# FNet mixing gated by a GLU: another load position for tiles five to eight, and other places for statistics, the fourth tile's turn and normalisations in the first block

## The chip, the cores and the metric

The kernel runs on one core of one Trainium2 chip. The metric is the device time of one execution in microseconds (us), and of several executions the median. The core has a matrix engine (TensorE, PE in the profile, with its weight loads as PEld), a vector engine (VectorE, DVE), a scalar engine (ScalarE, ACT), GpSimd (POOL) and SyncE (SP), which issues most of the loads. Each engine works through its own list of instructions in order and waits on semaphores for the others.

## The reference, cut to what matters

```python
x = A_x                                   # 1 x 2048 x 512
xn = _layernorm(x, axis=-1)
a = einsum("bsd,ed->bse", xn, dft_hid_re)
b = einsum("bsd,ed->bse", xn, dft_hid_im)
s = einsum("ts,bse->bte", dft_seq_re, a) - einsum("ts,bse->bte", dft_seq_im, b)
h = sigmoid(xn @ w_gate) * (xn @ w_up)    # 512 -> 1792
g = silu(h @ w_down)                      # 1792 -> 512
return x + s * g
```

## The kernel before, in words

The 2048 rows of x are 16 tiles of 128 rows, in two halves of eight (`KH` is 8). The 1792 hidden columns are seven groups of 256. The kernel goes over the halves and, inside each, over the groups; then come the sequence transform and the hidden transform. Every fp32 operand is split into a rounded part ("hi", written by ACT) and the rest ("lo", written by DVE), and a product is three matmuls: hi by hi, hi by lo and lo by hi.

The change lies in the first block, the function `start`, which handles the first half and the first group while its eight tiles are still coming in. All its instructions are put out by `begin`, in an order written by hand; each engine takes its own in that order. The matter of the first block is this:

- `fetch(i)` allocates a page for tiles i and i+1 and has SP load both. With `hold=True` DVE first writes one word into the page, so that the load waits until DVE has come to that point of its list.
- `loads[0]` and `loads[1]` are the first and the second weights, 512 KB each. `w_hi(f, j)` and `w_lo(f, j)` split them for feature half f.
- `norm_a(i)` computes a tile's statistics: two instructions on DVE (L155, L156) and two small ones on POOL (L157, L158). `norm_b(i)` normalises the tile with them on DVE (L163).
- `turn(i)` transposes a normalised tile with four instructions on PE (L176) into one of two "pd" banks. `keep_hi(i)` (ACT, L195), `keep_lo(i)` (DVE, L201) and `keep_raw(i)` (ACT, L187) take it out of the bank, in that order. So `turn(i)` waits for `norm_b(i)` and for `keep_raw(i - 2)`, which frees the bank.
- `chunk(q, f, order, between)` multiplies tiles 2q and 2q+1 with feature half f: three passes of eight matmuls of 256 columns (L553). It needs both tiles' hi parts for its first pass, their lo parts for another, the weights' lo parts for the third. `between` is run among the passes.
- `next_tile(i)` turns tile i, takes it out of its bank, and prepares later tiles.
- `gated(b, f)` is a sigmoid on ACT (L566) and a product on DVE (L567), put out when the two chunks of 512 rows are done; the function that it returns splits the result (ACT L273, DVE L274) and is called one chunk later as `left`.
- Four operand splits of the following block (ACT L66, DVE L67, and two sums at L118) are put among the last chunks.

The loop over the chunks, where most of the order is set, reads before the change:

```python
for q in range(4):
    for f in range(2):
        if f == 0:
            chunk(q, f, ((0, 0), (1, 0), (0, 1)))
            next_tile(2 * q + 2)
        else:
            chunk(q, f, ((0, 0), (0, 1), (1, 0)), lambda: next_tile(2 * q + 3))
        if left:
            left()
        left = gated(q // 2, f) if q % 2 else None
```

Tiles are counted from 0 in the code, so tile 3 is the fourth, and tiles five to eight are i = 4 to 7.

Of the kernel before, what the change touches and what calls it, by code (L numbers as in the profile page):

```python
# [20 lines left out]
KH = NS // NH  # L21
# [10 lines left out]
def fnet_glu_kernel(ctx: ExitStack, tc: tile.TileContext, x, x_t, c_re, c_im, w_h, w_gu, w_down, out):  # L32
# [9 lines left out]
    def page(shape, dtype=F32R):  # L42
        return pages.tile([P, *shape], dtype, name="page")

    def bank(tag):
        return banks.tile([P, 512], F32, name=tag, bufs=2 if tag == "pd" else 1)
# [77 lines left out]
    units = []  # L124
# [7 lines left out]
    def after(n, f):  # L132
        extra.setdefault(n, []).append(f)
# [7 lines left out]
    def fetch(i, hold=False):  # L141
        pg = page([2, D], F32)
        if hold:
            nc.vector.memset(pg[:, 0, :1], 0.0)
        for j in range(2):
            xs[i + j] = pg[:, j, :]
            nc.sync.dma_start(xs[i + j], x[(i + j) * P : (i + j + 1) * P, :])
# [3 lines left out]
    def norm_a(i):  # L151
        st = stat.tile([P, 6], F32, name="st")
        mv = stat.tile([P, 2], F32, name="mv")
        rs = stat.tile([P, 2], F32, name="rs")
        nc.vector.bn_stats(st, xs[i])  # L155
        nc.vector.bn_aggr(mv, st)  # L156
        nc.gpsimd.tensor_scalar(rs[:, 0:1], mv[:, 1:2], EPS, None, op0=ALU.add)  # L157
        nc.gpsimd.tensor_tensor(rs[:, 1:2], rs[:, 0:1], mhalf, op=ALU.pow)  # L158
        st_of[i] = mv, rs

    def norm_b(i):
        mv, rs = st_of.pop(i)
        nc.vector.tensor_scalar(xs[i], xs[i], mv[:, 0:1], rs[:, 1:2], op0=ALU.subtract, op1=ALU.mult)  # L163
# [9 lines left out]
    def turn(i):  # L173
        turned[i] = bank("pd").rearrange("p (d s) -> p d s", d=ND)
        for d in range(ND):
            nc.tensor.transpose(turned[i][:, d, :], xs[i][:, d * P : (d + 1) * P], ident)  # L176

    def place(i):
        h, b, o = i // 8, i % 8 // 4, i % 4
        return [(h, j, b) for j in range(2)], slice(o * P, (o + 1) * P)  # L180

    def keep_raw(i):
        keys, at = place(i)
        for j, k in enumerate(keys):
            if k not in xraw:
                xraw[k] = page([2, SB], F32)
            nc.scalar.activation(xraw[k][:, :, at], turned[i][:, 2 * j : 2 * j + 2, :], AF.Copy)  # L187

    def keep_hi(i):
        keys, at = place(i)  # L190
        for j, (h, _, b) in enumerate(keys):
            k = h, XK[j, b]
            if xop[k].at is None:
                xop[k].at = page([2, SB]), page([2, SB])
            nc.scalar.activation(xop[k].at[0][:, :, at], turned[i][:, 2 * j : 2 * j + 2, :], AF.Copy)  # L195

    def keep_lo(i):
        keys, at = place(i)
        for j, (h, _, b) in enumerate(keys):
            hi, lo = xop[h, XK[j, b]].at  # L200
            nc.vector.tensor_tensor(lo[:, :, at], turned[i][:, 2 * j : 2 * j + 2, :], hi[:, :, at].bitcast(F32), op=SUB)  # L201
# [3 lines left out]
    def x_sum(h, k):  # L205

        if (h, k) not in xsum:
            xsum[h, k] = page([2, SB], F32)
        a, b = {
            1: lambda: (xraw[h, 0, 1], xraw[h, 0, 0]),  # L210
            2: lambda: (xraw[h, 1, 1], xsum[h, 1]),
            3: lambda: (xraw[h, 1, 1], xraw[h, 0, 1]),
            4: lambda: (xraw[h, 1, 0], xsum[h, 2]),
        }[k]()
        nc.vector.tensor_tensor(xsum[h, k], a, b, op=SUB)
# [54 lines left out]
    def finish(h, hs, b, f, s):  # L270
        pg = page([2, SB])
        hs[f, b] = pg[:, 0, :], pg[:, 1, :]
        nc.scalar.activation(pg[:, 0, :], s, AF.Copy)  # L273
        return lambda: nc.vector.tensor_sub(pg[:, 1, :], s, pg[:, 0, :].bitcast(F32))  # L274
# [251 lines left out]
    def start(h, g):  # L526

        loads = [Load(w_gu[g, k], [2, 4 * P]) for k in range(2)]
        wdl = Load(w_down[g], [2, D])
        wd = [Parts([wdl], lambda f=f: wdl.load()[:, f, :], [D], joint=True) for f in range(2)]  # L530
        w, hs, ps = {}, {}, {}

        def w_hi(f, j):
            k, o = QUAD[f, j]
            both = page([2, 4 * P])
            w[f, j] = both[:, 0], both[:, 1]
            nc.scalar.activation(both[:, 0], loads[k].load()[:, o, :], AF.Copy)

        def w_lo(f, j):
            k, o = QUAD[f, j]  # L540
            nc.vector.tensor_tensor(w[f, j][1], loads[k].load()[:, o, :], w[f, j][0].bitcast(F32), op=SUB)

        def chunk(q, f, order, between=None):
            b, a = divmod(q, 2)
            if a == 0:
                for m in range(2):
                    ps[b, f, m] = bank("gu"[m] + ("bc", "ab")[b][f])
            at = slice(a * 2 * P, (a + 1) * 2 * P)
            for n, (u, v) in enumerate(order):
                for m in range(2):  # L550
                    for d in range(ND):
                        o = (2 * m + d % 2) * P
                        nc.tensor.matmul(  # L553
                            ps[b, f, m][:, at],
                            w[f, d // 2][u][:, o : o + P],
                            xop[h, XK[d // 2, b]].at[v][:, d % 2, at],
                            start=n == d == 0,
                            stop=n == 2 and d == ND - 1,
                            skip_group_check=True,
                        )  # L560
                if n == 0 and between is not None:
                    between()

        def gated(b, f):
            s = page([SB], F32)
            nc.scalar.activation(s, ps[b, f, 0], AF.Sigmoid)  # L566
            nc.vector.tensor_mul(s, s, ps[b, f, 1])  # L567
            return lambda: finish(h, hs, b, f, s)()

        def begin():  # L570
            idle = bank("gc")

            def busy(times, wide):
                for _ in range(times):
                    nc.tensor.matmul(idle[:, :wide], ones[:, :P], ones[:, :wide], start=True, stop=True)

            busy(10, 512)
            fetch(0)
            loads[0].load()
            norm_a(0)  # L580
            fetch(2, hold=True)
            loads[1].load()
            fetch(4)
            fetch(6)
            for p in units[0][0] + units[2][0]:
                p.load()
            wdl.load()
            norm_a(1)
            w_hi(0, 0)
            norm_b(0)  # L590
            turn(0)
            busy(2, 256)
            keep_hi(0)
            norm_b(1)
            turn(1)
            busy(4, 256)
            keep_hi(1)
            w_hi(0, 1)
            w_lo(0, 0)
            norm_a(2)  # L600
            w_lo(0, 1)
            norm_a(3)
            for i in range(2):
                keep_lo(i)
            w_hi(1, 0)
            w_hi(1, 1)
            norm_b(2)
            for i in range(2):
                keep_raw(i)
            w_lo(1, 0)  # L610
            norm_b(3)
            w_lo(1, 1)

            def next_tile(i):
                if i >= KH:
                    return
                turn(i)
                keep_hi(i)
                if 3 < i + 1 < KH:
                    norm_b(i + 1)  # L620
                keep_lo(i)
                if i + 2 < KH:
                    norm_a(i + 2)
                keep_raw(i)

            left = None
# [3 lines that stand above are left out]
                        chunk(q, f, ((0, 0), (1, 0), (0, 1)))  # L630
                        next_tile(2 * q + 2)
                    else:
                        chunk(q, f, ((0, 0), (0, 1), (1, 0)), lambda: next_tile(2 * q + 3))
                    if left:
                        left()
                    left = gated(q // 2, f) if q % 2 else None
                    n = 2 * q + f - 3
                    if 0 <= n < 4:
                        units[0 if n < 2 else 2][0][2 + n % 2].get()
            left()  # L640
            x_sum(h, 1)
            x_sum(h, 2)
            after(0, lambda: x_sum(h, 3))
            after(0, lambda: x_sum(h, 4))

        return (h, g, hs, wd), begin
# [313 lines left out]
    with tc.manual_schedule():  # L960
# [3 lines left out]
        for h in range(NH):  # L964
            n = len(units)
# [12 lines left out]
            if h == 0:  # L978
                n = len(units)
# [81 lines left out]
```

## Time and profile before

| what | value |
|---|---|
| median of 3 runs | 821.85 us (821.62 to 821.89) |
| the profiled execution: time, span | 822.36 us, 820.6 us |
| PE busy in the span | 809.8 us (99%) |
| DVE, ACT, POOL busy | 645.2, 490.9, 144.0 us |
| PE busy in the first 10, second 10, third 10 us | 8.08, 8.83, 9.25 us |
| granted PE clock | 0.999 |

The profiled execution is 0.51 us longer than the median of the runs and 1.76 us longer than its own span, which runs from the first to the last instruction. A row of the timeline gives the start in us, the length in us, the engine with line, operation and tiles, how many instructions are merged into it, and in brackets how long the engine had been idle and what ended that. The length of a matmul is modelled and overlaps the next one; the distance between starts tells the rate. A row of the chain of waits gives start, length and the work on the path to the end.

### The profile page before, as it was taken

The numbers are of one execution on the slowest core, as the hardware profiler recorded it, in microseconds if no ns is written. First come the engines' busy times: TensorE is split into PE (matmuls) and PEld (weight loads), VectorE is DVE, ScalarE is ACT, GpSimd is POOL, SyncE is SP. The second block draws the span as 40 slices with busy tenths as digits, with TensorE's granted clock in tenths as the row PEclk, the third lists the DMA queues.
The fourth block names the chain that finished last, engine by engine and source line by source line (L and its number), as shares of the span: only waits on it lengthen the run. The fifth ranks groups of instructions, "written<-read, shape, count | busy, mean of one in ns | idle before, by whom it ended". The sixth has DMA issues, their size and how long they took to land.

```text
span 820.6 us, 10472 instructions
## 1 busy us (share of the span) xinstructions
PE 809.8 (99%) x3686; PEld 673.2 (82%) x3686; DVE 645.2 (79%) x814; ACT 490.9 (60%) x762; POOL 144.0 (18%) x214
## 2 busy tenths in 40 slices
PE   8999999999999999999999999999999999999997
PEld 7988888888878888888888888888888888888786
DVE  6798867757788867876797796889888976988946
ACT  4666655655677888887787773544355545535441
POOL 2143422322111122212121100011101110002201
PEclk9999999999999999999999999999999999999999
DMA  8349999699677888998999997358937994799984
GB/s 317 144 170 401 272 257 285 186 321 309 163 175 165 228 179 214 251 200 199 280 291 311 265 347 271 134 209 309 310 146 287 341 394 150 253 316 395 304 275 77
DMA packets 59253, 207.27 MB, mean 253 GB/s; under 512 B 6592, under 2 KB 6848, under 8 KB 59200
## 3 DMA queue, kind: packets, MB, share of 16 engines
q0 software_dynamic: 25072, 87.57, 42.1%
q1 hardware_dynamic: 34128, 119.03, 40.2%
q8 instruction: 29, 0.48, 0.2%
q14 instruction: 24, 0.20, 0.1%
HBM read 122.16 MB, written 88.08 MB: 256 GB/s over the span
## 4 chain that ended last, share of the span: by engine, by line
PE 93%; DVE 3%; ACT 1%; DMA 1%; issue 1%; POOL 0%; SPq 0%; DVEq 0%
PE pd L70 6%; PE pd L71 6%; PE pd L72 6%; PE ga L70 5%; PE ga L72 5%; PE ua L72 5%; PE ua L71 5%; PE ga L71 5%; PE ua L70 5%; PE gc L70 3%; PE gc L72 3%; PE gc L71 3%; PE uc L72 3%; PE uc L70 3%; PE uc L71 3%; PE gb L72 3%
## 5 line engine op out<-in xcount | busy, mean ns | idle before, releaser
L67 DVE TENSOR_TENSOR page<-page 128x1024 fp32r<-128x1024 f32 (+1 forms) x340 | 322.0, 978 | 116.0 <-ACT page L66 114.5
L66 ACT ACTIVATE page<-page 128x1024 fp32r<-128x1024 f32 (+1 forms) x340 | 276.1, 859 | 91.8 <-DVE page L118 72.1
L118 DVE TENSOR_TENSOR page<-page 128x1024 f32<-128x1024 f32 (+2 forms) x184 | 169.2, 935 | 8.0 <-DMA page<-xn_part 5.9
L291 ACT ACTIVATE page<-pd 128x512 f32<-128x512 f32 x154 | 89.5, 595 | 62.7 <-PE pd L72 59.4
L295 POOL DMA_DIRECT2D g_part<-page x69 | 60.1, 889 | 277.2 <-ACT page L291 220.6
L70 PE MATMUL pd<-page 128*128 128x512 f32 x242 | 94.3, 390 | 0.8 <-DVE page L898 0.8
L71 PE MATMUL pd<-page 128*128 128x512 f32 x242 | 94.2, 389 | 0.0
L72 PE MATMUL pd<-page 128*128 128x512 f32 x242 | 94.2, 389 | 0.0
L70 PE MATMUL ga<-page 128*128 128x512 f32 x200 | 78.1, 391 | 0.8 <-ACT page L308 0.8
L72 PE MATMUL ga<-page 128*128 128x512 f32 x200 | 77.9, 390 | 0.0
L72 PE MATMUL ua<-page 128*128 128x512 f32 x200 | 77.9, 390 | 0.0
L71 PE MATMUL ga<-page 128*128 128x512 f32 x200 | 77.9, 389 | 0.0
L70 PE MATMUL ua<-page 128*128 128x512 f32 x200 | 77.9, 389 | 0.0
L71 PE MATMUL ua<-page 128*128 128x512 f32 x200 | 77.9, 389 | 0.0
L70 PEld LDWEIGHTS pd<-page 128*128 128x128 f32 x242 | 45.4, 188 | 10.7 <-issue 1.2
L72 PEld LDWEIGHTS pd<-page 128*128 128x128 f32 x242 | 45.4, 188 | 9.4
L71 PEld LDWEIGHTS pd<-page 128*128 128x128 f32 x242 | 45.4, 188 | 9.4
L70 PE MATMUL ub<-page 128*128 128x512 f32 (+1 forms) x126 | 48.3, 383 | 0.5 <-DVE page L940 0.5
L70 PE MATMUL gc<-page 128*128 128x512 f32 x124 | 48.6, 392 | 0.0
L71 PE MATMUL gc<-page 128*128 128x512 f32 x124 | 48.3, 390 | 0.0
L72 PE MATMUL gc<-page 128*128 128x512 f32 x124 | 48.3, 389 | 0.0
L70 PE MATMUL uc<-page 128*128 128x512 f32 x124 | 48.3, 389 | 0.0
(135 smaller groups left out, 1351.9 us busy)
## 6 DMA issues: line engine op xcount, KB each, us to landing
g_part<-page POOLq DMA_DIRECT2D x77, 512.0 KB, 7.8
page<-in_c_re_dram SPq DMA_DIRECT2D x36, 512.0 KB, 6.3
page<-f_part SPq DMA_DIRECT2D x36, 512.0 KB, 5.5
page<-in_c_im_dram SPq DMA_DIRECT2D x34, 512.0 KB, 6.0
page<-in_w_gu_dram SPq DMA_DIRECT2D x28, 512.0 KB, 7.6
f_part<-page POOLq DMA_DIRECT2D x28, 512.0 KB, 6.9
page<-in_w_down_dram SPq DMA_DIRECT2D x14, 512.0 KB, 8.7
page<-xn_part SPq DMA_DIRECT2D x14, 512.0 KB, 8.4
```

What stands on the lines that cost most here:

```text
L66: nc.scalar.activation(hi, src, AF.Copy)
L67: nc.vector.tensor_tensor(lo, src, hi.bitcast(F32), op=SUB)
L70: nc.tensor.matmul(ps, ws[0], ms[0], start=first, stop=False, skip_group_check=go_on)
L71: nc.tensor.matmul(ps, ws[0], ms[1], start=False, stop=False, skip_group_check=go_on)
L72: nc.tensor.matmul(ps, ws[1], ms[0], start=False, stop=last, skip_group_check=go_on)
L118: (engine or nc.vector).tensor_tensor(dst, a, b, op=op)
L291: nc.scalar.activation(pg[:, o, :], po, AF.Copy, scale=float(sign))
L295: nc.gpsimd.dma_start(g_part[i], pg, accum_op=ADD)
```

## The change

- The loads of tiles 4 to 7 move behind `norm_a(2)` and are held by DVE. With them move the loads behind them on SP's list: the two weights of the next group and the down weights (512 KB each).
- `norm_a(3)` moves behind `norm_b(2)`, and `norm_b(3)` behind both `w_lo` of the second weights.
- In the first chunk of feature half 1 the fourth tile's turn stands behind the second pass and no longer behind the first. In the later chunks of that half the turn stays behind the first pass.
- `norm_b(4)` to `norm_b(7)` leave `next_tile` and stand at the end of the loop's body, behind `left` and `gated`.

```diff
@@ chunk
             for n, (u, v) in enumerate(order):
+                if n and n - 1 in (between or {}):
+                    between[n - 1]()
...
-                if n == 0 and between is not None:
-                    between()
@@ begin
             loads[1].load()
-            fetch(4)
-            fetch(6)
-            for p in units[0][0] + units[2][0]:
-                p.load()
-            wdl.load()
             norm_a(1)
...
             norm_a(2)
+            for i in (4, 6):
+                fetch(i, hold=True)
+            for p in units[0][0] + units[2][0]:
+                p.load()
+            wdl.load()
             w_lo(0, 1)
-            norm_a(3)
...
             for i in range(2):
                 keep_raw(i)
+            norm_a(3)
             w_lo(1, 0)
+            w_lo(1, 1)
             norm_b(3)
-            w_lo(1, 1)
@@ next_tile
                 keep_hi(i)
-                if 3 < i + 1 < KH:
-                    norm_b(i + 1)
                 keep_lo(i)
@@ the loop
-                        chunk(q, f, ((0, 0), (0, 1), (1, 0)), lambda: next_tile(2 * q + 3))
+                        chunk(q, f, ((0, 0), (0, 1), (1, 0)), {int(q == 0): lambda: next_tile(2 * q + 3)})
...
                     left = gated(q // 2, f) if q % 2 else None
+                    if 3 < 2 * q + f + 3 < KH:
+                        norm_b(2 * q + f + 3)
```

## The prediction

> **What bounds the kernel now.** I read the chain that ended last, then PE's own waits over the whole run (those after the first, which is ahead of all work), then the timeline of the first block.
>
> ```profile
> PE 93%; DVE 3%; ACT 1%; DMA 1%; issue 1%; POOL 0%; SPq 0%; DVEq 0%
> ```
>
> ```profile
> PE pd L70 <- DVE page L898: 0.8, 1, 0.8
> PE ga L70 <- ACT page L308: 0.8, 1, 0.8
> PE pd L176 <- DVE page L163: 0.7, 1, 0.7
> PE gb L553 <- DVE page L201: 0.6, 1, 0.6
> PE pd L176 <- ACT page L187: 0.6, 1, 0.6
> PE ub L70 <- DVE page L940: 0.5, 1, 0.5
> ```
>
> PE is the bound almost everywhere. What any order of the first block can change is PE's waiting there; whatever PE loses or gains before about 37 us moves all that follows. Three waits lie where the change works: 0.6 on the lo parts (L201), 0.6 on a bank freed by ACT (L187), 0.7 on a normalised tile (L163). The change must remove these, and it may put new ones in their place.
>
> **The first two waits.** Timeline rows of the first 14 us, then rows of the chain and one of the page's groups that give PE's rate:
>
> ```profile
> 1.64 0.42 SPq L81 DMA_DIRECT2D page<-in_w_gu_dram  x1
> 5.05 0.43 SPq L81 DMA_DIRECT2D page<-in_w_gu_dram  x1
> 5.53 1.87 SPq L147 DMA_DIRECT2D page<-in_x_dram  x4
> 6.49 0.63 ACT L537 ACTIVATE page<-page 128x512 fp32r<-128x512 f32 x1 [4.26 <-DMA page<-in_w_gu_dram]
> 9.40 0.68 DVE L155 BATCH_NORM_STATS2 st<-page 128x6 f32<-128x512 f32 x1
> 10.22 1.39 DVE L201 TENSOR_TENSOR page<-pd,page 128x256 fp32r<-128x256 f32 x4
> 11.32 0.83 PE L553 MATMUL gb<-page 128*128 128x256 f32 x4 [0.60 <-DVE page L201]
> 11.45 1.15 ACT L537 ACTIVATE page<-page 128x512 fp32r<-128x512 f32 x2 [2.73 <-DMA page<-in_w_gu_dram]
> 11.52 0.54 DVE L163 TENSOR_SCALAR page<-page,mv,rs 128x512 f32<-128x512 f32 x1
> 13.20 0.66 PE L176 MATMUL pd<-ident,page 128*128 128x128 f32 x4 [0.57 <-ACT page L187]
> ```
>
> ```profile
> 19.08 0.48 PE gb L553 x4
> 19.56 0.48 PE ub L553 x4
> 37.66 0.23 PE ga L71
> ```
>
> ```profile
> L71 PE MATMUL pd<-page 128*128 128x512 f32 x242 | 94.2, 389 | 0.0
> ```
>
> A pass of eight takes 0.96. A matmul's row is longer than its share of PE's time: 389 ns against 0.23.
>
> Without norm_a(3) ahead of them, the lo parts start at 9.40 where L155 stood, not at 10.22: 0.82 earlier, more than the 0.60 that PE waited for them. That wait goes. The two held pages put two one-word writes into DVE's list; they fall where DVE waits for ACT's split of the first weights, so I cost them at nothing (if that cover is gone, no more than twice the 0.18 of L156, below).
>
> The turn at 13.20 waited for ACT: second weights landed 11.45, two splits, then the copies that free the bank, 1.75 in all. So this turn stands at the landing plus 1.75, or where PE and norm_b(2) allow it. PE alone allows 13.20 - 0.60 - 0.57, less 0.16 twice, because a row's modelled end hangs over by 0.389 - 0.23: 11.71. norm_b(2) moves up by the same 0.82, to 10.70, and ends at 11.24. The landing is the unknown. The first weights, with nothing issued behind them, took 6.49 - 1.64 = 4.85 from issue to use; the second, with the four tiles issued right behind, 11.45 - 5.05 = 6.40. The bounds are 9.90 and 11.45. I take 9.90, because the changed list gives the second weights the surroundings of the first: SP issues nothing more until DVE reaches the held pages' writes, about 0.8 ahead of the L155 at 9.40, at about 8.6. Then the turn comes at about 11.7, **1.5 earlier**; at the other end nothing is gained.
>
> [...]
>
> The tiles' loads go out from about 8.7, not 5.53.
>
> ```profile
> DMA to landing us min/median/max: 2.5/6.7/8.4
> ```
>
> By this row of L147 tile 4 lands between 11.2 and 17.1; DVE wants it for norm_a(4) at about 14.5. Only the rest of the second weights is ahead of it, so I take the lower half and no cost; at 17.1 it would cost 1.2 (DVE's 2.6 less what PE still has queued). The next weights and the down weights slip by some 3 us and are first split among the last chunks (L66): no cost.
>
> In the first chunk of half 1 one pass, 0.96, is left between the fourth tile's turn and the chunk that needs it, before it was two. norm_a(3), both w_lo and norm_b(3) are now ahead of keep_lo(2) on DVE, keep_raw(2) waits for that, and keep_hi(3) stands behind it on ACT. Between nothing and one ACT copy pair (0.66, below); I take **+0.1**, since the pass covers most of it.
>
> **The sixth tile's turn: a new wait.** Timeline rows:
>
> ```profile
> 19.88 0.60 PE L176 MATMUL pd<-ident,page 128*128 128x128 f32 x4
> 20.18 0.55 DVE L163 TENSOR_SCALAR page<-page,mv,rs 128x512 f32<-128x512 f32 x1 [0.99 <-POOL rs L158]
> 20.52 0.66 ACT L195 ACTIVATE page<-pd 128x256 fp32r<-128x256 f32 x2 [1.46 <-PE pd L176]
> 21.21 0.76 DVE L201 TENSOR_TENSOR page<-pd,page 128x256 fp32r<-128x256 f32 x2 [0.48 <-ACT page L195]
> 21.27 0.60 PE L176 MATMUL pd<-ident,page 128*128 128x128 f32 x4
> 21.88 0.68 DVE L155 BATCH_NORM_STATS2 st<-page 128x6 f32<-128x512 f32 x1
> 22.60 0.18 DVE L156 BATCH_NORM_AGGREGATE mv<-st 128x2 f32<-128x6 f32 x1
> 23.18 0.69 DVE L567 TENSOR_TENSOR page<-page,ub 128x512 f32<-128x512 f32 x1 [0.40 <-ACT page L566]
> 23.79 0.54 DVE L163 TENSOR_SCALAR page<-page,mv,rs 128x512 f32<-128x512 f32 x1
> ```
>
> Before, norm_b(5) runs at 20.18, ahead of keep_lo(4), and the sixth tile turns at 21.27, 1.39 behind the fifth. In the changed list norm_b(5) stands at the end of the body for (q, f) = (1, 0): behind keep_lo(4), norm_a(6) and the gated product. That is just the place that norm_b(6) has here, the L163 at 23.79. But the turn of the sixth tile keeps its place behind the first pass of the next chunk. DVE works in order, and its list from the fifth tile's turn is keep_hi on ACT (0.64 later), keep_lo (1.33), L155 (2.00), L156 (2.72), ACT's sigmoid and L567 (3.30), L163 (3.91 to 4.45). So the turn comes 4.5 behind the fifth and not 1.39: **+3.1**. Queued behind it on PE are two passes of the chunk and all else, and PE has nothing it could do first.
>
> **The eighth tile's turn: the same again.**
>
> ```profile
> 26.51 0.60 PE L176 MATMUL pd<-ident,page 128*128 128x128 f32 x4
> 27.14 0.66 ACT L195 ACTIVATE page<-pd 128x256 fp32r<-128x256 f32 x2
> 28.05 0.60 DVE L163 TENSOR_SCALAR page<-page,mv,rs 128x512 f32<-128x512 f32 x1
> 28.58 0.73 DVE L201 TENSOR_TENSOR page<-pd,page 128x256 fp32r<-128x256 f32 x2
> 28.81 0.63 PE L176 MATMUL pd<-ident,page 128*128 128x128 f32 x4 [0.75 <-DVE page L163]
> 29.35 0.66 ACT L187 ACTIVATE page<-pd 128x256 f32<-128x256 f32 x2 [1.55 <-DVE page L201]
> 29.89 0.63 ACT L273 ACTIVATE page<-page 128x512 fp32r<-128x512 f32 x1
> 30.56 0.69 DVE L274 TENSOR_TENSOR page<-page 128x512 fp32r<-128x512 f32 x1 [1.24 <-ACT page L273]
> ```
>
> Before, norm_b(7) at 28.05 is ahead of keep_lo(6), and the eighth tile turns 2.30 behind the seventh, 0.75 of it waiting. In the changed list it is behind keep_lo(6) and behind L274, which waits for L273, which on ACT follows keep_raw(6), which waits for keep_lo(6). From the seventh tile's turn: hi parts done 1.29, keep_lo from 1.32, keep_raw 0.77 later, L273 0.54 later, L274 0.67 later, L163 about 0.6 later and 0.6 long: 4.5, and the turn at 4.55. Against 2.30 that is **+2.25**, the removed 0.75 already in it. norm_b(6), behind the product that ends the chunk before, comes just in time for the seventh turn by the same spacings (0 to 0.3 late, I take 0).
>
> The chunk behind the eighth turn started at once on hi parts that had ACT splits ahead of them; those are done by then, which gives back some **0.15**.
>
> **Sum:** -1.5 + 0.1 + 3.1 + 2.25 - 0.15 = +3.8. The profiled execution would be 822.36 + 3.8 = 826.2 (span 824.4). It was 0.5 above the median of the runs, 821.85, so the median would be **825.6**. 0.2% of this kernel, about what a measurement can tell, is 1.6.
>
> **Rivals.**
> 1. *The second weights land no earlier.* For it: nothing in the trace shows that the tiles' loads held them up. Then the first gain is lost, the 0.1 too: +5.2, **827.0**. 0.33.
> 2. *PE starts cold after each long wait.* This row of the timeline shows it cold at the start: ten matmuls of 512 columns in 4.56, against the 0.23 each of the chain.
>
> ```profile
> 1.45 4.56 PE L575 MATMUL gc<-ones 128*128 128x512 f32 x10 [1.45 <-DVE ones L51]
> ```
>
> Half speed for such a stretch, 4.6 long, loses 2.3; after both waits 4.6: **830.2**. It decides if an idle time of 3.1 is long enough; the waits in this trace, up to 1.45, tell nothing of that. 0.07. [...]
> 3. *Lost time is regained.* PE's later waits, 0.8, 0.8 and 0.5, shrink because DVE and ACT, not held up as long, get ahead: at most 2.1, **823.5**. Against it: those chains begin at PE's own work. 0.05.
> 4. *Faster.* DVE reaches norm_b(5) and norm_b(7) within one pass, 1.39, of the turn before them, so that no new wait arises, and the three old ones go (0.76 + 0.73 + 0.9): -2.4, **819.4**. It needs keep_hi, keep_lo and the statistics alone, 2.72 by the rows, to take half that. 0.04; with rival 3 going further, 0.03 for no change.
>
> **How the numbers follow.** The forecast has 0.48, by the terms above. Forecast and first rival together are 0.81 and span 825.6 to 827.0; with 0 to 0.3 late on the seventh turn, the 0.36 of the two writes and the +0.1 going to 0.66, or each turn 0.5 sooner, the range is 824.6 to 827.8. Slower by over 0.2%: 0.48 + 0.33 + 0.07 + 0.05 = 0.93; faster 0.04; within 0.03.
>
> **What would show it.** Right: in PE's waits of the first block two on L163 of about 3 each, at about 20 to 23 and 29.5 to 32.8; the 0.6 on L201 gone; L537's second pair at 9.9 to 10.3 and the third tile's turn at about 11.7; PE's waits past 40 us as before. Wrong: no wait of over 1 us on L163, or L155 waiting for in_x loads, or passes of over 0.96 behind the waits.

## The result and the profile after

| | executions | median us | range | ratio to before |
|---|---|---|---|---|
| before | 6 | 821.87 | 821.62 to 822.30 | |
| after | 6 | 828.03 | 826.42 to 830.81 | 1.0081 (1.0063 to 1.0099) |

The changed kernel is slower by 6.2 us, where 3.8 were forecast; 828.03 lies 0.2 above the forecast's range. The six executions fall into three groups, and the mean granted clock of TensorE goes with them: 826.42 at 1.000; 827.83, 828.01 and 828.06 at 0.997 to 0.998; 830.23 and 830.81 at 0.994 to 0.995. The profiled execution is the one of 828.06, with a span of 826.3.

PE's own waits in the kernel after, of 0.5 us and more and without the one at the start (a wait's row: total us, times, longest):

```profile
PE pd L176 <- DVE page L163: 6.3, 3, 3.1
PE pd L70 <- DVE page L898: 0.8, 1, 0.8
PE ga L70 <- ACT page L308: 0.8, 1, 0.8
PE ub L70 <- DVE page L940: 0.5, 1, 0.5
```

The waits on L201 and L187 are gone, as the prediction said; those past 40 us are what they were. What grew is one row: turns waiting for a normalised tile, 0.7 before, 6.3 now. The timeline of the first block shows where (the chunk's matmul is L555 here, L553 before):

```profile
5.23 0.43 SPq L81 DMA_DIRECT2D page<-in_w_gu_dram  x1
10.01 1.16 ACT L537 ACTIVATE page<-page 128x512 fp32r<-128x512 f32 x2 [1.18 <-DMA page<-in_w_gu_dram]
11.76 0.66 PE L176 MATMUL pd<-ident,page 128*128 128x128 f32 x4
12.24 0.58 POOL L157 TENSOR_SCALAR rs<-mv 128x1 f32<-128x1 f32 x1 [2.88 <-DVE mv L156]
12.91 0.86 POOL L158 TENSOR_TENSOR rs<-rs,mhalf 128x1 f32<-128x1 f32 x1
13.81 0.55 DVE L163 TENSOR_SCALAR page<-page,mv,rs 128x512 f32<-128x512 f32 x1 [0.46 <-POOL rs L158]
14.50 0.63 PE L176 MATMUL pd<-ident,page 128*128 128x128 f32 x4 [0.18 <-DVE page L163]
16.04 0.78 PE L555 MATMUL gb<-page 128*128 128x256 f32 x4
19.05 0.60 PE L176 MATMUL pd<-ident,page 128*128 128x128 f32 x4
20.38 0.76 DVE L201 TENSOR_TENSOR page<-pd,page 128x256 fp32r<-128x256 f32 x2 [2.08 <-ACT page L195]
21.05 0.68 DVE L155 BATCH_NORM_STATS2 st<-page 128x6 f32<-128x512 f32 x1
22.35 0.69 DVE L567 TENSOR_TENSOR page<-page,ub 128x512 f32<-128x512 f32 x1 [0.40 <-ACT page L566]
22.96 0.54 DVE L163 TENSOR_SCALAR page<-page,mv,rs 128x512 f32<-128x512 f32 x1
23.65 1.09 PE L176 MATMUL pd<-ident,page 128*128 128x128 f32 x4 [3.04 <-DVE page L163]
24.39 1.20 PE L555 MATMUL gc<-page 128*128 128x256 f32 x4
26.88 0.64 PE L555 MATMUL uc<-page 128*128 128x256 f32 x4
30.23 0.60 PE L176 MATMUL pd<-ident,page 128*128 128x128 f32 x4
34.86 0.63 PE L176 MATMUL pd<-ident,page 128*128 128x128 f32 x4 [3.07 <-DVE page L163]
```

The reader can follow the forecast's list on DVE row by row: lo parts at 20.38, statistics at 21.05, gated product at 22.35, and only then the normalisation at 22.96 that the sixth turn waits for. That turn comes 4.60 us behind the fifth, the eighth 4.63 behind the seventh.

Something else stands behind the sixth turn: the same four transposes take 1.09 instead of 0.60, and a row of four of a pass takes 1.20, where it takes 0.64 from 26.88 on. The view by windows gives the clock (columns: stretch, its length, then busy us of PE, PEld, DVE, ACT and POOL with their instructions, granted clock, DMA share, GB/s):

```profile
23.00:23.50 0.50, 0.00 (x0) 0.00 (x0) 0.50 (x2) 0.00 (x0) 0.00 (x0) 0.69 0.97 385
23.50:26.00 2.50, 2.35 (x11) 2.38 (x12) 0.54 (x2) 0.66 (x2) 0.00 (x0) 0.50 0.24 97
26.00:26.50 0.50, 0.50 (x5) 0.50 (x4) 0.50 (x2) 0.25 (x1) 0.00 (x0) 0.50 0.00 0
26.50:27.00 0.50, 0.50 (x6) 0.50 (x5) 0.47 (x2) 0.50 (x3) 0.00 (x0) 0.90 0.00 0
```

The clock is halved while PE still waits, at about 23.2 (0.69 in that half us is 0.19 at full and 0.31 at half speed), and is full again at about 26.6: 3.4 us. Behind the eighth turn, which waited as long (3.07 against 3.04), it did not fall in this execution: it reads 1.00 from 32 to 38.

### The profile page after: what moved, and what is told of

Read it like the earlier page. It is cut to its first block, busy times and chain, and to the rows that moved or that the text cites. A ratio compares the mean times of both kernels' runs of the same rounds, so it can differ in the third digit from the quotient of the medians.

```text
span 826.3 us, 10474 instructions
## 1 busy us (share of the span) xinstructions
PE 811.3 (98%) x3686; PEld 674.4 (82%) x3686; DVE 645.3 (78%) x816; ACT 491.8 (60%) x762; POOL 144.6 (18%) x214
## 4 chain that ended last, share of the span: by engine, by line
PE 93%; DVE 4%; ACT 1%; issue 1%; POOL 0%; DMA 0%; DVEq 0%
PE pd L70 6%; PE pd L71 6%; PE pd L72 6%; PE ga L70 5%; PE ga L72 5%; PE ua L72 5%; PE ua L70 5%; PE ga L71 5%; PE ua L71 5%; PE uc L70 3%; PE gc L72 3%; PE gc L70 3%; PE uc L72 3%; PE gc L71 3%; PE uc L71 3%; PE gb L72 3%
## 5 line engine op out<-in xcount | busy, mean ns | idle before, releaser
L70 PE MATMUL gc<-page 128*128 128x512 f32 x124 | 48.6, 392 | 0.0
L70 PE MATMUL uc<-page 128*128 128x512 f32 x124 | 48.3, 389 | 0.0
L72 PE MATMUL gc<-page 128*128 128x512 f32 x124 | 48.3, 389 | 0.0
L72 PE MATMUL uc<-page 128*128 128x512 f32 x124 | 48.3, 389 | 0.0
```

What stands on the lines that cost most here:

```text
L70: nc.tensor.matmul(ps, ws[0], ms[0], start=first, stop=False, skip_group_check=go_on)
L72: nc.tensor.matmul(ps, ws[1], ms[0], start=False, stop=last, skip_group_check=go_on)
```

## The experiments

Each kernel was timed beside the kernel before on the same chip; that one's medians were 821.62, 821.81 and 821.80 in the three sets.

**Normalisations back.** The changed kernel with one part undone.

```diff
@@ next_tile
                 keep_hi(i)
+                if 3 < i + 1 < KH:
+                    norm_b(i + 1)
                 keep_lo(i)
@@ the loop
-                    if 3 < 2 * q + f + 3 < KH:
-                        norm_b(2 * q + f + 3)
```

> The changed kernel, with only the normalisations norm_b(4) to norm_b(7) put back into next_tile. Theory A (the loss is the place of norm_b(5) and norm_b(7) behind work that needs the turn before, plus PE's clock after the long waits): no wait of PE on L163 above 0.9 us, granted clock 1.00 in the first block, the gain of the loads and statistics is left: about 1.0 below the kernel before, 820.9 (820.5 to 821.3). Rival B (the loss comes from the held loads or from the other pages that they get): still 3 or more above the kernel before, 825 or more.

Measured: 821.51 (821.03 to 822.28, 11 executions), ratio 0.9998 (0.9990 to 1.0007), clock 0.999 to 1.000. Its waits on L163:

```profile
PE pd L176 <- DVE page L163: 0.9, 2, 0.6
```

The whole loss comes with the places of the four normalisations. But what is left of the change, the loads, the statistics and the fourth turn, is 0.1 faster by the medians, which the interval does not tell from nothing; the 1.4 of the forecast lies outside it.

**Normalisations alone.** The kernel before, with only that part done (the diff above the other way round).

> The kernel before, with only the normalisations norm_b(4) to norm_b(7) moved to the end of the loop's body. Theory A: two waits of PE of 3.0 to 3.2 us on L163, at the sixth and the eighth tile's turn; +3.1 + 2.25 - 0.15 = +5.2 without any drop of the clock, 827.1, and 828.5 to 831 in executions where the clock drops after one or both waits. Rival B: within 0.5 of the kernel before.

Measured: 830.37 (828.18 to 831.16, 4 executions), ratio 1.0109 (1.0094 to 1.0124), clock 0.994 to 0.997.

```profile
PE pd L176 <- DVE page L163: 6.1, 2, 3.1
```

The same two waits with none of the other edits, and the clock at 0.997 or below in every execution, where the kernel before has 0.998 to 1.000.

**Waits filled.** The changed kernel, with 24 constant matmuls put ahead of the sixth and of the eighth turn, into a bank that is written anew later.

```diff
@@ next_tile
+                if i in (5, 7):
+                    fill = bank("ga" if i == 5 else "gc")
+                    for _ in range(24):
+                        nc.tensor.matmul(fill[:, :256], ones[:, :P], ones[:, :256], start=True, stop=True)
                 turn(i)
```

> The changed kernel, with 24 matmuls of 256 columns on constants ahead of the sixth and of the eighth tile's turn (2.9 us each, into a bank that is free then; their result is not used). They fill PE's waits without ending them later. Theory A (the clock drops because PE is idle for about 3.1 us): clock 1.00 throughout, runs within 0.6 of each other, at the lowest time of the changed kernel, 826.4 (826.0 to 826.9). Rival C (the matmuls behind the wait are slow for another reason, or the clock drops whatever PE does): the same times and the same spread as the changed kernel, 826.4 to 830.8, median 828.

Measured: 826.45 (826.25 to 826.77, 5 executions), ratio 1.0058 (1.0046 to 1.0071), clock 0.998 to 1.000.

```profile
20.44 3.03 PE L620 MATMUL ga<-ones 128*128 128x256 f32 x24
23.64 0.63 PE L176 MATMUL pd<-ident,page 128*128 128x128 f32 x4 [0.17 <-DVE page L163]
```

The sixth turn comes at the same time as in the kernel after, 23.64 against 23.65, so the filler costs nothing and saves nothing of the wait itself. Yet the time is that of the one undisturbed execution of the kernel after, and the spread is 0.5 instead of 4.4. So the spread and some 1.6 us of the median are the clock, and by this run the clock falls because PE stands still. Against the kernel with the normalisations back, on the same chip, the two waits cost 826.45 - 821.51 = 4.94.

**Waits lengthened.** Two writes of 0.49 us on DVE ahead of each of the two normalisations.

```diff
@@ the loop
                     if 3 < 2 * q + f + 3 < KH:
+                        if 2 * q + f + 3 in (5, 7):
+                            for _ in range(2):
+                                nc.vector.memset(ones.bitcast(F32), 1.0)
                         norm_b(2 * q + f + 3)
```

> The changed kernel, with two more writes of 0.49 us on DVE ahead of norm_b(5) and of norm_b(7), so that each of PE's two waits is about 1.0 longer, 4.1. [...] Rival D (a drop comes by chance, whatever the length of the wait): 2.0 above the changed kernel, median 830, with the same spread of over 4 us. Rival C: 2.0 above and no drop that follows the waits.

Measured: 833.48 (833.20 to 833.60, 4 executions), ratio 1.0143 (1.0129 to 1.0157), clock 0.992 in all.

```profile
24.75 1.09 PE L176 MATMUL pd<-ident,page 128*128 128x128 f32 x4 [4.06 <-DVE page L163]
38.01 1.08 PE L176 MATMUL pd<-ident,page 128*128 128x128 f32 x4 [4.10 <-DVE page L163]
```

```profile
20.00:24.50 4.50, 0.69 (x6) 0.48 (x5) 3.38 (x8) 1.57 (x5) 0.79 (x2) 0.86 0.89 345
24.50:28.00 3.50, 3.25 (x16) 3.29 (x17) 1.50 (x5) 1.31 (x5) 0.00 (x0) 0.50 0.01 4
28.00:32.00 4.00, 4.00 (x28) 4.00 (x27) 2.58 (x5) 1.54 (x4) 2.43 (x4) 0.74 0.33 114
```

Now both turns run at half speed in the profiled execution, the other three have the same mean clock, and the spread is gone again. Two drops at the 1.4 to 2.2 seen in the kernel after, and 2.0 for the writes, would give 826.4 + 2.0 + 2.8 to 4.4 = 831.2 to 832.8. The time is 0.7 above that: one drop costs (833.48 - 826.45 - 2 x 1.02) / 2 = 2.5, since the half-speed stretch is twice as long. From the windows it is 1.26 + 3.5 + 2.08 = 6.8 us.

**The turn one pass later.** The changed kernel, with the next tile's turn behind the second pass in all rounds, so that the waits get shorter.

```diff
-                        chunk(q, f, ((0, 0), (0, 1), (1, 0)), {int(q == 0): lambda: next_tile(2 * q + 3)})
+                        chunk(q, f, ((0, 0), (0, 1), (1, 0)), {1: lambda: next_tile(2 * q + 3)})
```

> The changed kernel with the next tile's turn behind the second pass of the odd chunks in every round, not only in the first: the sixth and the eighth turn come one pass later, so that the normalisation has that much less to be waited for. Nothing is left out. Theory A (a turn that waits costs its wait, and the clock only drops when TensorE stands still for about 3 us or more): the wait ahead of the sixth and the eighth turn shrinks from 3.04 and 3.07 us to 2.1 to 2.4 each, a wait of up to 0.9 us may come ahead of the seventh, the clock stays at 1.0 in all runs, and the runs agree within 0.4 us: 825.4 us (824.9 to 826.0). Theory B (any wait of TensorE of some 2 us can halve the clock): runs spread over 1.5 us or more as in the changed kernel, clock 0.995 to 0.998 in most, 827 to 829.

Measured: 827.68 (825.88 to 827.93, 5 executions), ratio 1.0065 (1.0052 to 1.0079), clock 0.994 to 0.998.

```profile
23.55 0.63 PE L176 MATMUL pd<-ident,page 128*128 128x128 f32 x4 [2.08 <-DVE page L163]
33.95 0.63 PE L176 MATMUL pd<-ident,page 128*128 128x128 f32 x4 [2.11 <-DVE page L163]
```

```profile
24.50:25.00 0.50, 0.50 (x7) 0.50 (x5) 0.10 (x1) 0.37 (x2) 0.00 (x0) 0.90 0.02 8
25.00:28.00 3.00, 3.00 (x17) 3.00 (x16) 2.54 (x6) 2.18 (x5) 1.35 (x3) 0.50 0.00 0
28.00:28.50 0.50, 0.50 (x5) 0.50 (x4) 0.50 (x2) 0.00 (x0) 0.50 (x2) 0.69 0.00 0
```

The waits shrank as theory A said, and theory A fell: the clock is at 0.994 to 0.996 in four of the five executions, and in the profiled one it drops behind both turns (the fifth, 825.88 at 0.998, leaves open if it dropped once or not at all). The drop comes late: PE is back at work at 23.55, at full speed (the turn takes 0.63), and only at 24.9 does the clock halve, for 0.1 + 3.0 + 0.3 = 3.4 us. So a standstill of 2.1 us was enough here, and PE was not idle when the clock fell.

**Waits filled in part.** Two kernels with the filler above, with 12 and with 18 matmuls instead of 24.

> The changed kernel with 12 constant matmuls of 256 columns ahead of the sixth and of the eighth turn, instead of the 24 that filled both waits: each shortens its wait of 3.04 and 3.07 us by some 1.4 us to about 1.6 us, and the turns come no earlier or later by it. Nothing is left out. Theory A (the clock only halves when TensorE has stood still for about 3 us): 826.4 us (826.1 to 826.8), clock 1.0 in all runs. Theory B (a standstill of under 2 us within a stretch of some 3.4 us is enough in some runs): a median of 827 to 829.5 with a spread of over 1.5 us.

> The changed kernel with 18 constant matmuls of 256 columns ahead of the sixth and of the eighth turn: each wait is left with some 0.9 us, and the turns stay where they are. Nothing is left out. Theory A: 826.4 us (826.1 to 826.8), clock 1.0 in all runs. Theory B: the same, if the kernel before is a guide, whose wait of 0.75 us left the clock at 0.999 to 1.0; a spread of over 1.5 us would say that under 1 us of standstill is enough.

Measured: 826.46 (826.42 to 826.75, 5 executions), ratio 1.0058 (1.0046 to 1.0071), clock 1.000 in all; and 826.66 (826.36 to 826.75, 5 executions), ratio 1.0059 (1.0046 to 1.0071), clock 0.999 to 1.000. PE's waits on L163, of the first and of the second:

```profile
PE pd L176 <- DVE page L163: 3.4, 3, 1.6
```

```profile
PE pd L176 <- DVE page L163: 1.7, 2, 0.9
```

Five executions with two waits of 1.6 each, and no drop; against 2.1, where at least four of five had one. Theory A's border of 3 is too high by the kernel with the later turn. Theory B's drops did not come at 1.6; a wait of 1.88 in the last kernel below shows that they can come under 2.

**The loads alone.** The kernel before, with the loads of tiles five to eight and what follows them on SP moved behind `norm_a(2)` and held, as in the change, and nothing else.

> The kernel before with one part of the change alone: the loads of tiles five to eight, of the next weights and of the first down weights are issued behind the third tile's statistics, and everything else stays. Nothing is left out. Theory C (the loads issued behind the second weights never held them up; their landing at 11.45 us in the profile of before was that one execution): the same as before, 821.4 to 821.9. Theory D (the loads held the second weights up by 1.5 us, as the prediction took it): the third turn comes at 11.7 us and the time falls by 0.7 to 1.5: 820.1 to 820.9.

Measured: 821.57 (821.30 to 822.04, 11 executions), ratio 0.9996 (0.9987 to 1.0005): no difference that can be told.

```profile
10.92 1.15 ACT L537 ACTIVATE page<-page 128x512 fp32r<-128x512 f32 x2 [1.83 <-DMA page<-in_w_gu_dram]
11.67 0.83 PE L553 MATMUL gb<-page 128*128 128x256 f32 x4 [0.61 <-DVE page L201]
12.83 0.60 PE L176 MATMUL pd<-ident,page 128*128 128x128 f32 x4
```

The third turn comes at 12.83 without any wait of its own; what is ahead of it on PE waited for L201. So an earlier landing alone does not bring the turn to 11.7.

**The kernel before again,** for a second profile.

> The kernel before once more, for a second profile. Theory C (the landing of the second weights at 11.45 us was one execution's): they land at 10.0 to 10.5 us, the wait of 0.57 us ahead of the third turn is gone, and the third turn comes at 12.3 to 12.6 us instead of 13.20. Theory D (the loads behind them hold them up each time): landing at 11.2 to 11.6, third turn at 13.0 to 13.3.

Measured: 822.87, one execution.

```profile
12.38 1.15 ACT L537 ACTIVATE page<-page 128x512 fp32r<-128x512 f32 x2 [3.56 <-DMA page<-in_w_gu_dram]
14.13 0.66 PE L176 MATMUL pd<-ident,page 128*128 128x128 f32 x4 [1.31 <-ACT page L187]
```

Neither theory had this: the landing is later still. From SP's issue to ACT's use of the second weights it takes 6.40, 7.15 and 5.50 us in three executions with the tiles' loads right behind (before, before again, normalisations alone), and 4.27 to 5.78, median 4.73, in the eleven profiled ones with the loads held. The two groups overlap: the longest with the loads held, 5.78, is above the shortest without. Theory C is wrong on this landing. Theory D is wrong on the time, by the kernel with the loads alone. Both profiled executions of the kernel before lie above its median, by 0.5 and 1.1; in normalisations alone, whose list is the same up to there, the weights were used at 10.67 and the third turn came at 12.48. So 13.20 need not be the usual place of that turn.

**Sums put off.** The changed kernel with the normalisations back, the last of them ahead of the gate, and with the work of VectorE between the seventh and the eighth turn put off by one chunk.

```diff
@@ next_tile
+                if 3 < i + 1 < KH - 1:
+                    norm_b(i + 1)
                 keep_lo(i)
@@ the loop
+                    if (q, f) == (2, 0):
+                        continue
                     if left:
                         left()
+                    if (q, f) == (1, 1):
+                        norm_b(KH - 1)
...
-                    if 3 < 2 * q + f + 3 < KH:
-                        norm_b(2 * q + f + 3)
                     n = 2 * q + f - 3
-                    if 0 <= n < 4:
-                        units[0 if n < 2 else 2][0][2 + n % 2].get()
+                    for n in (1, 2) if n == 2 else (n,):
+                        if 0 <= n < 4:
+                            units[0 if n < 2 else 2][0][2 + n % 2].get()
```

> The changed kernel with the normalisations back in the turns (the one ahead of the eighth tile behind the gate of the chunk before it), and with the work of VectorE that stands between the seventh tile's turn and the eighth's (the sums of the fifth chunk's tail and one split) put off by one chunk. Nothing is left out. Theory A (the path to the first block's end goes through the turns, and 0.24 and 0.62 us are left ahead of the fourth and the eighth turn): the wait ahead of the eighth turn goes, and with it 0.6 to 0.9 us; 820.4 us (820.1 to 820.8). Rival: what is put off is waited for a chunk later, or the end of the block is set by the splits of VectorE and not by the turns: 821.3 to 821.9, the same as before.

Measured: 821.92 (821.73 to 822.38, 11 executions), ratio 1.0003 (0.9994 to 1.0011). The rival held:

```profile
39.43 2.48 DVE L215 TENSOR_TENSOR page<-page 128x1024 f32<-128x1024 f32 x2
42.57 0.50 PE L72 MATMUL pd<-page 128*128 128x512 f32 x1 [1.03 <-DVE page L67]
```

The first block ends sooner (PE's first matmul behind it starts at 35.35, against 36.54 in the profile with the normalisations back), and PE runs into a new wait of 1.03: VectorE, with two sums of 2.48 together, has not yet split the down weights.

**Down weights first.** The same with those splits ahead of the two sums.

```diff
             left()
+            for v in wd:
+                v.get()
             x_sum(h, 1)
             x_sum(h, 2)
```

> The kernel of the put-off sums (normalisations back in the turns, the sums of the fifth chunk's tail one chunk later) with the splits of the first down weights ahead of the two sums of 2.48 us on VectorE, for which TensorE waited 1.03 us at 42.6 us there. Nothing is left out. Theory A (the gain of the first block was given back in that one wait): the wait goes, and the time falls by 0.7 to 1.0 us to 820.9 to 821.2; below the kernel before by 0.5 to 1.0. Rival: the two sums, now 1.4 us or more later, are waited for in the third unit, and it stays at 821.7 to 822.0.

Measured: 823.52 (823.03 to 824.21, 10 executions), ratio 1.0023 (1.0014 to 1.0033). The rival again, and worse than it said:

```profile
11.78 0.60 PE L176 MATMUL pd<-ident,page 128*128 128x128 f32 x4
16.07 0.78 PE L555 MATMUL gb<-page 128*128 128x256 f32 x4
43.37 2.00 ACT L66 ACTIVATE page<-page 128x1024 fp32r<-128x1024 f32 x2 [3.31 <-DVE page L215]
45.91 0.50 PE L70 MATMUL ga<-page 128*128 128x512 f32 x1 [1.88 <-ACT page L308]
```

The wait of 1.03 is gone, and one of 1.88 stands 3 us further on: ACT's splits and copies, held up by the sums. In these two kernels what the first block gains is lost at a wait behind it. That VectorE as a whole sets the pace there, in whatever order, is argued and not shown.

**Statistics back.** The same, with `norm_a(3)` in its place of before, ahead of the lo parts.

```diff
             w_lo(0, 1)
+            norm_a(3)
             for i in range(2):
                 keep_lo(i)
...
             for i in range(2):
                 keep_raw(i)
-            norm_a(3)
```

> The same kernel as the one with the splits of the first down weights ahead, with the statistics of the fourth tile back in their place of before (behind the second split of the second weights' half, ahead of the third tile's sums) and all else the same. Nothing is left out. Theory E (the early part gives back some 0.4 us between the third turn and the chunk behind the fourth, because GpSimd has the fourth tile's deviation late): the wait of 0.24 us ahead of the fourth turn goes, the distance from the third turn to that chunk falls from 4.2 to 4.3 us to 3.8, and the time falls by 0.3 to 0.5 against the kernel without this step. Rival (VectorE as a whole sets this stretch, in whatever order): the distance stays at 4.2 or grows, and the time is the same within 0.2 us.

Measured: 824.21 (823.24 to 824.74, 7 executions), ratio to the kernel before 1.0027 (1.0015 to 1.0038); against the kernel without this step 0.7 slower by the medians, with overlapping ranges and intervals. The first rows are of the start, the last three of a wait further on and of the clock behind it.

```profile
9.92 1.15 ACT L537 ACTIVATE page<-page 128x512 fp32r<-128x512 f32 x2 [1.08 <-DMA page<-in_w_gu_dram]
11.41 0.83 PE L555 MATMUL gb<-page 128*128 128x256 f32 x4 [0.58 <-DVE page L201]
12.55 0.60 PE L176 MATMUL pd<-ident,page 128*128 128x128 f32 x4
16.28 0.64 PE L555 MATMUL gb<-page 128*128 128x256 f32 x4
```

```profile
45.97 0.50 PE L70 MATMUL ga<-page 128*128 128x512 f32 x1 [1.88 <-ACT page L308]
```

```profile
46.00:47.00 1.00, 1.00 (x4) 0.86 (x5) 1.00 (x2) 0.41 (x1) 0.00 (x0) 0.94 0.00 0
50.00:51.00 1.00, 1.00 (x5) 0.79 (x4) 1.00 (x3) 0.00 (x0) 1.00 (x2) 0.85 0.47 193
```

Half of theory E held: the distance from the third turn to the chunk behind the fourth is 16.28 - 12.55 = 3.73, against 16.07 - 11.78 = 4.29. But the third turn is 0.77 later, with the weights in at 9.92, because the lo parts wait for the statistics. The move gains 0.77 ahead of the third turn and gives 0.56 back behind it: 0.2 is left.

This profiled execution, 824.57 at 0.997, also has a drop of the clock: half speed from 46.88 to 50.30, 3.4 us, behind the wait of 1.88. The three executions at 0.999 have a median of 823.50, the seven at 0.999 of the kernel without this step 823.47. So the 0.7 between the medians goes with the clock; a gain or loss of the step itself can't be told.

## Why the prediction was right and where it was wrong

**The two new waits: right.** Place, cause and size are as forecast: 4.60 and 4.63 behind the turn before, where 4.5 and 4.55 were given. Both terms with the 0.15 given back came to 5.2; the experiments put them at 4.94. The seventh turn was not late.

**The clock: the step that failed.** The sum had no term for it, and rival 2 got 0.07. It struck in five of six executions. As a mechanism the rival was right; its price, 2.3 for each wait, lies between the 1.4 to 2.2 seen (from 826.42 to 827.83 to 828.06, and to 830.23 and 830.81 if these two had a drop behind each wait; they were not profiled) and the 2.5 of the longer waits. The stretch behind a wait of 3.04 is 3.4 long and not the 4.6 of the start; there the profile's clock column reads 1.00, and only the rate of the rows is halved (ten matmuls of 512 columns in 4.64 in the kernel after, 0.46 each, against 0.23). What failed is the rival's condition: the waits of before, up to 1.45, left open where the border was, and the forecast set it above 3.1, the author's estimate, which no run bears out: the clock fell behind waits of 2.08 and 2.11, once behind 1.88, and not behind 1.61. Nor does the length alone tell: in one execution it fell behind 3.04 and not behind 3.07.

**The early gain: mis-sized.** The forecast had -1.5 + 0.1; by the kernel with the normalisations back it is -0.1. Two reasons. The third turn did come at 11.76, as forecast, but 13.20, from which the 1.5 was counted, belongs to an execution with a late landing; in normalisations alone, with the same list up to there, it is 12.48, and from there the gain is 0.7. And the move of the statistics, which gains 0.77 there, gives back 0.56 behind the turn, where 0.1 was put: the fourth tile's deviation is now made on GpSimd at 12.2 to 13.8, DVE waits 0.46 for it, and PE 0.18 ahead of the fourth turn. That turn comes 2.74 behind the third, with the statistics back 2.35 (12.55 to 14.90); the rest of the 0.56 lies behind it. The prediction looked at the copies behind the turn alone and gave GpSimd no price.

**The landing: right, and without an effect on the time that can be told.** Issue to use went from 6.40 to 4.78, where 4.85 was forecast, and most of the other profiles with held loads bear it out (median 4.73). Rival 1 fell on the landing; what it said of the time, that the first gain is lost, came true in another way, and that is luck. With four tiles right behind, the weights took 5.50 to 7.15. What the rows show is a later landing, not the mechanism.

**The sum,** with what the runs put in the place of each term: -0.1 + 4.9 + 1.6 for the clock = 6.4, against 6.2 measured. The sign rests on the two waits, which held. The size was missed by the clock and by the early gain, 1.6 and 1.3, both to the same side. Rivals 3 and 4 fell: the waits past 40 us are unchanged, and none of the versions tried was shown to be faster than the kernel before.

**How much standstill is enough.** The profiles answer it in part. The clock fell in or behind waits of 1.88 (statistics back), 2.08 and 2.11 (later turn), 3.04 (the kernel after, and normalisations alone, where the turn behind it takes 1.09), 4.06 and 4.10 (longer waits). It did not fall behind waits of 1.88 (down weights first), 3.07 (after) and 3.08 (normalisations alone, turn 0.63), nor behind the 1.61 and 1.55 that 12 matmuls as filler left. So waits of 1.88 and of about 3.05 are on both lists, and no run shows what decides there.

The half speed lasted 3.4 us in four stretches: 23.19 to 26.60 in the kernel after, 24.90 to 28.31 and 35.1 to 38.6 with the later turn (0.52 from 35.0 to 38.5, 0.99 from there to 42.0), 46.88 to 50.30 with the statistics back. Behind the wait of 4.06 it lasted 6.8, from 23.24 to 30.08. All this is read from single profiled executions, with modelled ends of matmuls; no run moved a wait of one length to another time.

## What to carry to other kernels

Price a new wait of the matrix engine twice: by its length, and by what a half clock behind it may cost. Here the clock fell in or behind waits of 1.88 to 4.10 us, not behind each of them, and cost 1.4 to 2.5 us behind those of 3 to 4; if the wait can't be avoided, matmuls that nobody reads, put into it, took the second part away here. When a step is moved ahead on an engine that works in order, the steps that it overtakes come later; look for who waits for those before the gain is booked (here 0.56 of 0.77 was given back). A start counted from one profiled execution should be held against the median of the runs or a second profile: here 13.20, where another execution of the same list has 12.48, became a gain that was not to be had.

## What was not expected of the hardware

- The granted clock halved over 1 us after a standstill, with PE at work again (later turn): standstill 21.47 to 23.55, drop at about 24.9. The row that is slow is then not the row that waited.
- Standstills of 1.6 us: no drop in 5 executions with two each. Of 1.88: a drop in one profile (statistics back), none in another (down weights first). Of 2.1: a drop in at least 4 of 5, by a mean clock of 0.994 to 0.996. Of 3.05: in 5 of 6 (after, 0.994 to 0.998) and 4 of 4 (normalisations alone, 0.994 to 0.997). Of 4.1: two in the profiled one, 6.8 us long behind the first, and the same clock of 0.992 in all 4.
- Constant matmuls that fill the wait cost nothing that the runs show: the turn behind them comes at 23.64 against 23.65.
- A 512 KB load took between 4.27 and 7.15 us from issue to use in the same place of one kernel family, the two longest with four tile loads issued right behind it.
